# First layer of experts 1 to 7 over two token units at once: 512-column matmuls in place of pairs of 256-column ones

## The chip, the cores and the metric

The kernel runs on one core of a Trainium2 chip. The metric is the device time of one execution in microseconds (us); lower is better. All profile times are from one execution recorded by the hardware profiler. Engines: PE is the matrix engine, PEld its weight load, DVE the vector engine, ACT the scalar engine, POOL GpSimd, SP the sync engine, which here only issues DMAs.

## The reference

Linear attention over 8 batches and 8 heads, 576 positions of 64 numbers, then a mixture of 8 experts in which every token goes through every expert, weighted by a Sinkhorn-balanced matrix P:

```python
q_p, k_p = phi(q), phi(k)                       # phi(x) = elu(x) + 1
kv  = einsum('bhsd,bhse->bhde', k_p, v);  z = sum(k_p, axis=2)
x   = (q_p @ kv) / (q_p . z + 1e-6)             # reshaped to 4608 x 512
P   = exp(x @ w_gate - max)                     # 4608 x 8
for _ in range(8):                              # Sinkhorn
    P /= P.sum(1, keepdims=True) + 1e-9
    P /= P.sum(0, keepdims=True) + 1e-9
    P *= N / E
out = 0
for e in range(8):
    h = relu(x @ w1[e])                         # 512 -> 1024
    out += P[:, e:e+1] * (h @ w2[e])            # 1024 -> 512
```

## The kernel before, in words

**How the order comes about.** Nothing is issued while the program text is read. Every step is a task given to a list scheduler (`_Plan`, L18 to L119) with an engine, an estimated cost, its dependences, a priority, and the buffers that it takes or uses. `S_.run()` then places the tasks engine by engine. Two things written by hand go before that: a table of ranks (`ranks`, L1026 to L1163), which sets priorities and sometimes the engine of single tasks, and a chain of dependences (`order`, `final`, L1009 ff.) that fixes the sequence of PE's products for experts 1 to 7.

**Front.** 16 attention blocks load k, q and v (mostly on SP's queue), compute phi, kv and the quotient, and leave x transposed as `xT` in SBUF, in f16. Sinkhorn runs on PE, DVE and ACT beside expert 0.

**Tokens and experts.** The 4608 tokens are 9 units of 512. For expert 0 the first five units use plain matmuls (layer 1 at L583, layer 2 at L809); the last four units, and all units of experts 1 to 7, use a seven-product scheme in the manner of Strassen for layer 1 (`block7`, L658). Layer 2 of experts 1 to 7 also has seven products (`unit`, L884), apart from the very last unit, whose layer 2 is plain (`unit_plain`, L809, L793).

**The combinations.** The scheme splits the 512 input features and the 512 tokens of a unit in halves. The products need sums of weight blocks (`W`, made by `combos` on DVE, four per expert), and four combinations of x per unit. `x_blocks` (L598 to L636) makes the latter on DVE and writes raw x and combinations to a DRAM tile `xd[g]` with three DMAs on SP (L606, L607, L636). `x_load` (L648) brings 896 KB per unit back as one tile `xs` with one DMA, in two buffers.

**Layer 1 of a unit.** `pair(gi)` is run for gi = 0 and 1. Each has seven products m1 to m7 of four 256-column matmuls (L703): two blocks p of 128 hidden features times two halves c of the contraction. In the order names they are a1 to a7 and b1 to b7; A is the next unit's a. ACT seeds a bank from another (L715), copies two (`s2` L722, `s5` L729) and writes h11 and h21 with relu (L732, L735); DVE writes h12 and h22, an add with relu (L738). m4 waits for h22, as it adds to the same bank.

**Layer 2 of a unit.** Four sums `S` of h on DVE (L900), four sums `T` of w2 per expert (DVE), seven products y1 to y7 of eight 256-column matmuls (L927), and evacuations `acc += P * y`: ten on DVE (L941), two through ACT (L948) and POOL (L951), and a seed copy (L962). In expert 7 finished rows are written out by `out_dma` on SP (L778).

PE's order for unit u in experts 1 to 7, with y of the unit before:

```python
order = "y1 y5 y2 a7 y6 y3 a4 b1 b5 y7 b6 b3 b2 b7 A1 A5 y4 b4 A6 A3 A2".split()
final = "y1 y5 y2 y6 a7 y3 a4 b1 b5 y7 b6 b3 b2 b7 y4 b4".split()
```

Of the kernel before, what the change touches and what calls it, by code (L numbers as in the profile page):

```python
# [122 lines left out]
def kernel(  # L123
# [32 lines left out]
    hpool = ctx.enter_context(tc.tile_pool(name="hpool", bufs=2))  # L156
# [9 lines left out]
    NXB = 7 * 512  # L166
    NL = 4
    NF = 8
    NX = 5
    MG = 99  # L170
    xd = [dpool.tile([P, NXB], FP16, tag=f"xd{g}", name=f"xd{g}") for g in range(NG)]
# [20 lines left out]
    p_T, p_S, p_W, p_xs, p_xst, p_s2, p_s5 = (S_.pool(2) for _ in range(7))  # L192
# [343 lines left out]
    accp = []  # L536
    Zt = [None, None]

    def f_close(_):
        front.close()  # L540
        accp.append(ctx.enter_context(tc.tile_pool(name="accp", bufs=1)))
        for g in range(NA, NG):
            acc[g] = accp[0].tile([P, 4, 512], FP32, tag=f"acc{g}", name=f"acc{g}")
        accp.append(ctx.enter_context(tc.tile_pool(name="combo", bufs=2)))
        zps = ctx.enter_context(tc.tile_pool(name="zps", bufs=1, space=PSUM))
        for i, n in enumerate(("ye2", "ye3")):
            Zt[i] = zps.tile([P, 2, 256], FP32, tag=n, name=f"Z{n}")
# [12 lines left out]
    def layer1(e, g):  # L560
# [6 lines left out]
        def f_ha(_):  # L567
            gh["tile"] = hpool.tile([P, NFT, 512], FP16, tag="h", name="h")
# [29 lines left out]
    def x_blocks(g):  # L598
# [6 lines left out]
        def f_raw(_):  # L605
            nc.sync.dma_start(out=xd[g][:, 0:512].rearrange("p (c t) -> p c t", c=2), in_=xT[:, 0:2, t0:t0 + 256])  # L606
            nc.sync.dma_start(out=xd[g][:, 512:1536].rearrange("p (c t) -> p c t", c=2), in_=xT[:, 2:4, t0:t0 + 512])  # L607
        last = first = None
        for i in range(3):
            def f_T(_, i=i):  # L610
                if i == 0 and early:
                    h_ = (len(p_xse["order"]) - 1) % 2
                    gt_["tile"] = (acc[NA - 1][:, 2 * h_:2 * h_ + 2, :].bitcast(FP16)
                                   .rearrange("p a (b c t) -> p (a b) c t", b=2, c=2))
                elif i == 0:
                    gt_["tile"] = accp[1].tile([P, 4, 2, 256], FP16, tag="xst", name="xst")
# [18 lines left out]
        def f_st(_):  # L635
            nc.sync.dma_start(out=xd[g][:, 1536:NXB], in_=gt_["tile"].rearrange("p i c t -> p (i c t)"))  # L636
# [4 lines left out]
        x_users.append(out_[1])  # L641
# [4 lines left out]
    xst_of, xse_done = {}, []  # L646

    def x_load(e, g):  # L648
        gr = S_.grp(p_xs)

        def fn(_):
            gr["tile"] = accp[1].tile([P, NXB], FP16, tag="xs", name="xs")
            nc.sync.dma_start(out=gr["tile"], in_=xd[g])
        ti = add(("sp", 0.1), fn, acq=[gr], deps=xd_done[g] + [t_close, xs_prev[0]], prio=e * NG + g)
        xs_prev[0] = ti
        return gr, add(("dma", 3.0), lambda _: None, deps=[ti], use=[gr], prio=e * NG + g, lat=2.6)

    def block7(e, g, gW, tW):  # L658
        gw1, tw1, gw2, tw2 = w_t[e]
        ui = e * NG + g  # L660
        gxs, txs = xst_of[g][:2] if e == 0 else x_load(e, g)
        gh = S_.grp(p_h)
        th = [[], []]
        t0 = 512 * g

        def f_ha(_):
            gh["tile"] = hpool.tile([P, NFT, 512], FP16, tag="h", name="h")
        tha = add(("none", 0.0), f_ha, deps=[prev_hq[0]], acq=[gh], prio=ui - 400.0)

        def A(i, j, gi):  # L670
            return lambda p, c: gw1["tile"][:, 2 * (j - 1) + c, ts(4 * (i - 1) + 2 * gi + p, P)]

        def W(i, gi):
            return lambda p, c: gW["tile"][:, i - 1, c, ts(2 * gi + p, P)]

        def Bx(o, w):
            return lambda c: gxs["tile"][:, o + w * c:o + w * c + 256]

        def T(i):
            return Bx(1536 + 512 * (i - 1), 256)  # L680
        B11, B21, B22 = Bx(0, 256), Bx(512, 512), Bx(768, 512)
        if e == 0:
            def Bt(c0, t):
                return lambda c: xT[:, c0 + c, t:t + 256]

            def T(i):
                return lambda c: gxs["tile"][:, i - 1, c, :]
            B11, B21, B22 = Bt(0, t0), Bt(2, t0), Bt(2, t0 + 256)

        def pair(gi):  # L690
            gX, gR, gZ, gs2, gs5 = (S_.grp(p) for p in (p_hq, p_att, p_ye[3], *((p_e2, p_e5) if e == 0 else (p_s2, p_s5))))
            kx = {id(gX): (hqp, "hq"), id(gR): (aps, "att")}
            f0 = 2 * gi

            def pm(lhs, rhs, g_, first, deps, pr):
                def f_m(_):
# [3 lines left out]
                    dst = Zt[1] if g_ is gZ else g_["tile"]  # L700
                    for p in range(2):
                        for c in range(2):
                            nc.tensor.matmul(dst[:, p, :], lhsT=lhs(p, c), rhs=rhs(c),  # L703
                                             start=(first and p == 0 and c == 0), stop=(c == 1), skip_group_check=True)
                return add(("pe", 0.436), f_m, deps=deps, acq=[g_] if first else [], use=[g_, gw1, gW, gxs],
                           prio=ui + (-2.0 if ui == NG else 0.35) + 0.35 * gi + pr)

            def hd(fh, t):
                return gh["tile"][:, 4 * fh + f0:4 * fh + f0 + 2, 256 * t:256 * t + 256]

            def acts(fn, deps, use, acq=()):
                return add(("act", 0.6), fn, deps=deps, use=use, acq=acq, prio=ui - 400.0 + 0.1 * gi)
# [4 lines left out]
            def f_s2(_):  # L717
                if e == 0:
                    gs2["tile"] = acc[NG - 1][:, (len(p_e2["order"]) - 1) % 2, :].rearrange("p (a b) -> p a b", a=2)
                else:  # L720
                    gs2["tile"] = accp[2].tile([P, 2, 256], FP32, tag="s2", name="s2")
                nc.scalar.copy(out=gs2["tile"], in_=gX["tile"])  # L722

            def f_s5(_):
                if e == 0:
                    gs5["tile"] = acc[NG - 1][:, 2 + (len(p_e5["order"]) - 1) % 2, :].rearrange("p (a b) -> p a b", a=2)
                else:
                    gs5["tile"] = accp[2].tile([P, 2, 256], FP32, tag="s5", name="s5")
# [16 lines left out]
            m1 = pm(A(1, 1, gi), B11, gX, True, tw1 + [txs, prev_hq[0], t_zt], 0.0)  # L745
            prev_hq[0] = m1
            a1 = acts(f_seed, [m1], [gX], [gZ])
            m5 = pm(W(1, gi), T(1), gR, True, [m1, tW], 0.05)
            a5 = acts(f_s5, [m5, x_closed[0] if e > 0 else t_close], [gR], [gs5])
            m2 = pm(A(1, 2, gi), B21, gZ, False, [a1], 0.15)  # L750
            th[0].append(acts(f_h11, [m2, tha], [gZ, gh]))
            m6 = pm(W(2, gi), T(2), gX, False, [a1, tW], 0.08)
            a2 = acts(f_s2, [m6, x_closed[0] if e > 0 else t_close], [gX], [gs2])
            m3 = pm(W(4, gi), B22, gR, False, [a5], 0.12)
            th[1].append(add(("dve", 0.69), f_h12, deps=[m3, a2, tha], use=[gR, gs2, gh], prio=ui - 400.0))
            m7 = pm(W(3, gi), T(3), gX, False, [a2], 0.14)
            d22 = add(("dve", 0.69), f_h22, deps=[m7, a5, tha], use=[gX, gs5, gh], prio=ui - 402)
            th[1].append(d22)
            m4 = pm(A(2, 2, gi), T(4), gX, False, [d22], 0.16)
            for n, t in zip("1234567", (m1, m2, m3, m4, m5, m6, m7)):  # L760
                if e == 0:
                    x_users.append(t)
                else:
                    pe_id[(ui, f"{'ab'[gi]}{n}")] = t
            if e > 0:
                pe_id[(ui, f"{'ab'[gi]}22")] = d22
            th[0].append(acts(f_h21, [m4, tha], [gX, gh]))
        pair(0)
        pair(1)
        return gh, th  # L770
# [10 lines left out]
    def unit_plain(e, g, gW=None, tW=None):  # L781
        gw1, tw1, gw2, tw2 = w_t[e]
        gh, th = layer1(e, g) if gW is None else block7(e, g, gW, tW)
        gy = [S_.grp(p_ye[tt % 2]) for tt in range(4)]
        ty = [None] * 4
        cuts = []
        for c in range(2 if e > 0 else 0):
            gc = S_.grp((p_ye[0], p_hq)[c])

            def f_yc(_, c=c, gc=gc):  # L790
                gc["tile"] = (yps, hqp)[c].tile([P, 256], FP32, tag=("ye0", "hq")[c], name="yc")
                for f in range(NFT):
                    nc.tensor.matmul(gc["tile"], lhsT=gh["tile"][:, f, 0:P], rhs=gw2["tile"][:, f, 256 * c:256 * c + 256],  # L793
# [9 lines left out]
        for tt in range(1 if e > 0 else 0, 4):  # L803
            for half in range(2):
                def f_y(_, half=half, tt=tt):
                    if half == 0:
                        gy[tt]["tile"] = yps.tile([P, 512], FP32, tag=f"ye{tt % 2}", name=f"ye{tt % 2}")
                    for f in range(4 * half, 4 * half + 4):
                        nc.tensor.matmul(gy[tt]["tile"], lhsT=gh["tile"][:, f, ds(P * tt, P)], rhs=gw2["tile"][:, f, :],  # L809
# [4 lines left out]
                if e > 0:  # L814
                    pe_id[f"z{tt}{half}"] = ty[tt]
        for c, t in enumerate(cuts):
# [35 lines left out]
    def combos(e):  # L852
        gw1, tw1, gw2, tw2 = w_t[e]
        gT, gW = S_.grp(p_T), S_.grp(p_W)
        tW = tT = None
        if e == 0:
            gT = None
        for i in range(4):
            def f_W(_, i=i):
                if i == 0:  # L860
                    gW["tile"] = accp[1].tile([P, 4, 2, 512], FP16, tag="W", name="W")
                w, W = gw1["tile"], gW["tile"]
                a0, a1, op = [(w[:, 0:2, 512:1024], w[:, 2:4, 512:1024], ALU.add),
                              (W[:, 0], w[:, 0:2, 0:512], ALU.subtract),
                              (w[:, 0:2, 0:512], w[:, 0:2, 512:1024], ALU.subtract),
                              (w[:, 2:4, 0:512], W[:, 1], ALU.subtract)][i]
                nc.vector.tensor_tensor(out=W[:, i], in0=a0, in1=a1, op=op)
            tW = add(("dve", 0.685), f_W, deps=tw1 + [t_close, tW, pe_id.get((NG * (e - 1) + i + 1, "b22"))], acq=[gW] if i == 0 else [], use=[gw1, gW],
                     prio=-900.0 if e > 1 else 4.5)
        for i in range(4 if e > 0 else 0):  # L870
            def f_T(_, i=i):
                if i == 0:
                    gT["tile"] = accp[2].tile([P, 4, 4, 256], FP16, tag="T", name="T")
                w, T = gw2["tile"], gT["tile"]
                a0, a1, op = [(w[:, 0:4, 256:512], w[:, 0:4, 0:256], ALU.subtract),
                              (w[:, 4:8, 256:512], T[:, 0], ALU.subtract),
                              (w[:, 4:8, 256:512], w[:, 0:4, 256:512], ALU.subtract),
                              (w[:, 4:8, 0:256], T[:, 1], ALU.subtract)][i]
                nc.vector.tensor_tensor(out=T[:, i], in0=a0, in1=a1, op=op)
# [321 lines left out]
```

## Time and profile before

| what | value |
|---|---|
| three runs | 962.19, 963.14, 965.29 us |
| median | 963.14 us |
| profiled execution | span 960.4 us from its first to its last instruction; no other time of it is recorded |
| granted PE clock | 1.000 |
| PE busy | 954.2 us (99%), 8833 instructions |
| weight loads on PE | 803.7 us (84%) |
| DVE, ACT, POOL busy | 773.4 us (81%), 572.4 us (60%), 114.1 us (12%) |
| DMA moved | 121.99 MB in 46420 packets |

The span is 2.7 us below the median of the runs. Busy times of PE overlap, since matmuls are pipelined: the cost of a matmul is the distance between the starts of neighbours, not its duration.

### The profile page before, as it was taken

The numbers are of one execution on the slowest core, as the hardware profiler recorded it, in microseconds if no ns is written. First come the engines' busy times: TensorE is split into PE (matmuls) and PEld (weight loads), VectorE is DVE, ScalarE is ACT, GpSimd is POOL, SyncE is SP. The second block draws the span as 40 slices with busy tenths as digits, with TensorE's granted clock in tenths as the row PEclk, the third lists the DMA queues.
The fourth block names the chain that finished last, engine by engine and source line by source line (L and its number), as shares of the span: only waits on it lengthen the run. The fifth ranks groups of instructions, "written<-read, shape, count | busy, mean of one in ns | idle before, by whom it ended". The sixth has DMA issues, their size and how long they took to land.

```text
span 960.4 us, 21585 instructions
## 1 busy us (share of the span) xinstructions
PE 954.2 (99%) x8833; PEld 803.7 (84%) x8833; DVE 773.4 (81%) x1527; ACT 572.4 (60%) x1034; POOL 114.1 (12%) x163
## 2 busy tenths in 40 slices
PE   9999999999999999999999999999999999999998
PEld 4666676688888888888888888888888888888886
DVE  6998889878887888878887888878887888877775
ACT  6897755855555555555555555555555555555553
POOL 4100000011111111111111100111111111111110
PEclk9999999999999999999999999999999999999999
DMA  9987962252227222452227222272226321235554
GB/s 317 345 315 259 277 195 77 44 122 78 78 77 165 78 77 78 113 130 77 78 78 164 79 78 78 81 162 74 68 71 136 93 78 74 78 100 164 166 162 114
DMA packets 46420, 121.99 MB, mean 127 GB/s; under 512 B 4208, under 2 KB 18288, under 8 KB 46320
## 3 DMA queue, kind: packets, MB, share of 16 engines
q1 hardware_dynamic: 30576, 96.22, 30.1%
q0 software_dynamic: 15344, 23.87, 12.9%
q8 instruction: 69, 1.13, 0.5%
q10 hardware_dynamic: 400, 0.52, 0.2%
q14 instruction: 31, 0.25, 0.1%
HBM read 119.69 MB, written 17.69 MB: 143 GB/s over the span
## 4 chain that ended last, share of the span: by engine, by line
PE 95%; DMA 2%; ACT 2%; DVE 0%; issue 0%; POOL 0%; ACTq 0%; DVEq 0%
PE ye L927 34%; PE hq L703 24%; PE att L703 12%; PE ye L809 7%; PE Zye L703 6%; PE Zye L927 6%; PE hq L583 3%; DMA kqin<-in_k_dram 2%; ACT e L285 1%; PE xt_ps L413 1%; PE kv_ps L330 1%; PE num_ps L397 1%; PE qt_ps L358 1%; ACT h L587 0%; PE lg_ps L432 0%; PE den_ps L373 0%
## 5 line engine op out<-in xcount | busy, mean ns | idle before, releaser
L941 DVE SCALAR_TENSOR_TENSOR acc<-ye,P_sb,acc 128x256 f32<-128x256 f32 x620 | 267.3, 479 | 128.1 <-PE ye L927 127.6
L703 PEld LDWEIGHTS <-W 128*128 128x128 f16 x2144 | 209.8, 98 | 26.8 <-issue 0.2
L927 PEld LDWEIGHTS <-S 128*128 128x128 f16 x1984 | 194.1, 98 | 22.5
L927 PE MATMUL ye<-T,S 128*128 128x256 f16 x1488 | 192.8, 273 | 0.0
L703 PEld LDWEIGHTS <-w 128*128 128x128 f16 x1608 | 157.4, 98 | 20.1 <-issue 0.7
L735 ACT ACTIVATE h<-hq 128x512 f16<-128x512 f32 x134 | 80.1, 597 | 146.2 <-PE hq L703 143.3
L951 POOL TENSOR_TENSOR acc<-acc,st 128x256 f32<-128x256 f32 x124 | 87.3, 724 | 619.9 <-ACT st L948 609.2
L927 PEld LDWEIGHTS <-h 128*128 128x128 f16 x1488 | 145.6, 98 | 16.8
L703 PE MATMUL att<-xs,W 128*128 128x256 f16 x1008 | 151.2, 273 | 0.0
L703 PE MATMUL hq<-xs,W 128*128 128x256 f16 x1008 | 151.2, 273 | 0.0
L703 PE MATMUL hq<-xs,w 128*128 128x256 f16 x1008 | 140.9, 273 | 0.3 <-DVE h L738 0.3
L732 ACT ACTIVATE h<-Zye 128x512 f16<-128x512 f32 x134 | 80.1, 598 | 42.6 <-PE Zye L703 42.6
L948 ACT ACTIVATE st<-Zye,P_sb 128x256 f32<-128x256 f32 x124 | 51.9, 470 | 78.0 <-PE Zye L927 78.0
L900 DVE TENSOR_TENSOR S<-h 128x1024 f16<-128x1024 f16 x124 | 85.4, 689 | 13.7 <-ACT h L735 13.7
L738 DVE CUSTOM_DVE_ANT_0 h<-att,s 128x512 f16<-128x512 f32 x126 | 86.7, 688 | 11.7 <-ACT s L722 11.1
L722 ACT COPY s<-hq 128x512 f32<-128x512 f32 x126 | 73.6, 584 | 36.3 <-PE hq L703 36.3
L715 ACT COPY Zye<-hq 128x512 f32<-128x512 f32 x134 | 78.0, 582 | 17.8 <-PE hq L703 17.7
L738 DVE CUSTOM_DVE_ANT_0 h<-hq,s 128x512 f16<-128x512 f32 x126 | 86.7, 688 | 0.6 <-PE hq L703 0.6
L809 PE MATMUL ye<-w,h 128*128 128x512 f16 x312 | 76.6, 379 | 0.0
L703 PE MATMUL Zye<-xs,w 128*128 128x256 f16 x504 | 75.6, 273 | 0.0
L729 ACT COPY s<-att 128x512 f32<-128x512 f32 x126 | 74.6, 592 | 0.0
L927 PE MATMUL ye<-w,h 128*128 128x256 f16 x496 | 64.3, 273 | 0.0
(109 smaller groups left out, 949.7 us busy)
## 6 DMA issues: line engine op xcount, KB each, us to landing
xs<-xd SPq DMA_DIRECT2D x63, 896.0 KB, 4.6
w<-in_moe_w_dram POOLq DMA_DIRECT2D x14, 1024.0 KB, 11.5
out_dram<-acc SPq DMA_DIRECT2D x67, 128.0 KB, 2.4
kqin<-in_k_dram SPq DMA_DIRECT2D x12, 576.0 KB, 5.2
kqin<-in_q_dram SPq DMA_DIRECT2D x12, 576.0 KB, 6.6
vin<-in_v_dram SPq DMA_DIRECT2D x12, 576.0 KB, 7.3
xd<-acc SPq DMA_DIRECT2D x5, 512.0 KB, 4.9
kqin<-in_k_dram POOLq DMA_DIRECT2D x4, 576.0 KB, 10.5
```

The lines of the kernel that those rows point to most:

```text
L703: nc.tensor.matmul(dst[:, p, :], lhsT=lhs(p, c), rhs=rhs(c), start=(first and p == 0 and c == 0), stop=(c == 1), skip_group_check=True)
L715: nc.scalar.copy(out=Zt[1], in_=gX["tile"])
L722: nc.scalar.copy(out=gs2["tile"], in_=gX["tile"])
L729: nc.scalar.copy(out=gs5["tile"], in_=gR["tile"])
L732: nc.scalar.activation(out=hd(0, 0), in_=Zt[1], func=AF.Relu)
L735: nc.scalar.activation(out=hd(1, 0), in_=gX["tile"], func=AF.Relu)
L738: nc.vector._custom_dve(TENSOR_ADD_SAT, out=dst, in0=ps, in1=sb, s0=3.0e38, s1=0.0)
L809: nc.tensor.matmul(gy[tt]["tile"], lhsT=gh["tile"][:, f, ds(P * tt, P)], rhs=gw2["tile"][:, f, :], start=(f == 0), stop=(f == NFT - 1))
L900: nc.vector.tensor_tensor(out=Sx[:, i], in0=a0, in1=a1, op=op)
L927: nc.tensor.matmul(bank(g_)[:, s, :], lhsT=lhs(s, kk), rhs=rhs(kk), start=(new and s == 0 and kk == 0), stop=(kk == 3), skip_group_check=True)
L941: nc.vector.scalar_tensor_tensor(out=dst(), in0=bank(g_)[:, s, :], scalar=P_sb[:, gg, e:e + 1], in1=dst(), op0=ALU.mult, op1=ALU.add)
L951: nc.gpsimd.tensor_tensor(out=dst(), in0=dst(), in1=gst["tile"], op=ALU.add)
```

## The change

- In experts 1 to 7, units 0 to 7 of layer 1 are computed two at a time. A double unit has four pairs instead of two times two. One product of a pair is one block of 128 hidden features (no p loop) times two contraction halves, with 512 columns: 256 tokens of each of the two units. Unit 8 of each expert remains single.
- h of four units is kept in one tile `h4` with four places. Layer 2 stays per unit, but lags two units behind layer 1 instead of one.
- `xd` now holds a pair of units with the seven pieces contiguous. `x_blocks` writes it with seven DMAs per unit (1 + 2 raw, 4 combinations), and `x_load` fetches seven pieces per double unit (256 KB each; 128 KB for unit 8) into a ring of nine tiles.
- `W` and `S` become rings of single tiles (6 and 4), and `T` a ring of 8 in the space that held expert 0's h.
- The last unit's plain layer 2 is interleaved with the seven products of unit 7, and uses other PSUM banks.
- The table of ranks is new, in the front as well.

The core of the diff:

```diff
-    xd = [dpool.tile([P, NXB], FP16, tag=f"xd{g}", name=f"xd{g}") for g in range(NG)]
+    ND = NG // 2
+    xd = [dpool.tile([P, 7, 2, 2 if d < ND else 1, 256], FP16, tag=f"xd{d}", name=f"xd{d}") for d in range(ND + 1)]
...
-    p_T, p_S, p_W, p_xs, p_xst, p_s2, p_s5 = (S_.pool(2) for _ in range(7))
+    p_xst, p_s2, p_s5 = (S_.pool(2) for _ in range(3))
+    p_T, p_W, p_S, p_xs = S_.pool(8), S_.pool(6), S_.pool(4), S_.pool(NXR)
+    p_h4 = [S_.pool(1) for _ in range(4)]
...
         def f_raw(_):
-            nc.sync.dma_start(out=xd[g][:, 0:512].rearrange("p (c t) -> p c t", c=2), in_=xT[:, 0:2, t0:t0 + 256])
-            nc.sync.dma_start(out=xd[g][:, 512:1536].rearrange("p (c t) -> p c t", c=2), in_=xT[:, 2:4, t0:t0 + 512])
+            nc.sync.dma_start(out=xd[g // 2][:, 0, :, g % 2, :], in_=xT[:, 0:2, t0:t0 + 256])
+            for b in range(2):
+                nc.sync.dma_start(out=xd[g // 2][:, 1 + b, :, g % 2, :], in_=xT[:, 2:4, t0 + 256 * b:t0 + 256 * b + 256])
...
         def f_st(_):
-            nc.sync.dma_start(out=xd[g][:, 1536:NXB], in_=gt_["tile"].rearrange("p i c t -> p (i c t)"))
+            for i in range(4):
+                nc.sync.dma_start(out=xd[g // 2][:, 3 + i, :, g % 2, :], in_=gt_["tile"][:, i])
...
     def x_load(e, g):
-        gr = S_.grp(p_xs)
-
-        def fn(_):
-            gr["tile"] = accp[1].tile([P, NXB], FP16, tag="xs", name="xs")
-            nc.sync.dma_start(out=gr["tile"], in_=xd[g])
...
+        d = g // 2
+        out_ = {}
+        for b in (0, 3, 4, 2, 1, 5, 6):
+            gr = S_.grp(p_xs)
+
+            def fn(_, gr=gr, b=b):
+                gr["tile"] = accp[1].tile([P, 2, 2 if d < ND else 1, 256], FP16, tag="xs", name="xs", bufs=NXR)
+                nc.sync.dma_start(out=gr["tile"], in_=xd[d][:, b])
...
                     dst = Zt[1] if g_ is gZ else g_["tile"]
+                    if two:
+                        for c in range(2):
+                            nc.tensor.matmul(dst.rearrange("p a b -> p (a b)"), lhsT=lhs(0, c), rhs=X(b)(c),
+                                             start=(first and c == 0), stop=(c == 1), skip_group_check=True)
+                        return
                     for p in range(2):
                         for c in range(2):
-                            nc.tensor.matmul(dst[:, p, :], lhsT=lhs(p, c), rhs=rhs(c),
+                            nc.tensor.matmul(dst[:, p, :], lhsT=lhs(p, c), rhs=X(b)(c),
                                              start=(first and p == 0 and c == 0), stop=(c == 1), skip_group_check=True)
...
-        pair(0)
-        pair(1)
-        return gh, th
+        for gi in range(4 if two else 2):
+            pair(gi)
+        return ghs, th
...
     def unit(e, g, gW, tW, gT, tT):
...
-        gh, th = block7(e, g, gW, tW)
+        if g % 2 == 0:
+            h_of[0] = block7(e, g, gW, tW)
+        gh, th = h_of[0]
+        gh = gh[g % 2]
...
-    final = "y1 y5 y2 y6 a7 y3 a4 b1 b5 y7 b6 b3 b2 b7 y4 b4".split()
+    final = ("y1 y5 y2 a7 y6 y3 a4 b1 b5 y7 b6 b3 b2 b7 y4 Y1 b4 Y5 Y2 Y6 Y3 "
+             "z30 Y7 z31 z20 Y4 z21 z10 z11 z00 z01").split()
```

(Y is the layer 2 of the unit before the last one, z the plain layer 2 of the last unit.)

## The prediction

> **What bounds the kernel now.** I read the page's first two parts first: does one engine fill the span, and in which slices does it not?
>
> ```profile
> span 960.4 us, 21585 instructions
> PE 954.2 (99%) x8833; PEld 803.7 (84%) x8833; DVE 773.4 (81%) x1527; ACT 572.4 (60%) x1034; POOL 114.1 (12%) x163
> ...
> PE   9999999999999999999999999999999999999998
> ...
> PEclk9999999999999999999999999999999999999999
> DMA  9987962252227222452227222272226321235554
> ```
>
> PE is busy everywhere, at full clock; DVE has a fifth of the span free; the DMA engines are full only in the first five slices (0 to 120 us). A share cannot say whether PE is ever late, so next come the windows (columns: length, then busy time and count of PE, PEld, DVE, ACT, POOL, then clock, DMA share, GB/s):
>
> ```profile
> 0.00:60.00 60.00, 58.31 (x603) 34.11 (x604) 49.26 (x103) 46.39 (x64) 14.23 (x24) 1.00 1.02 332
> 60.00:120.00 60.00, 59.58 (x704) 38.02 (x702) 51.94 (x112) 49.01 (x80) 2.09 (x3) 1.00 0.88 274
> ...
> 450.00:550.00 100.00, 100.00 (x919) 89.63 (x917) 80.94 (x156) 56.67 (x106) 12.98 (x18) 1.00 0.36 103
> ...
> 850.00:960.40 110.40, 106.28 (x948) 92.50 (x946) 79.36 (x153) 56.33 (x106) 11.28 (x16) 1.00 0.54 145
> ```
>
> From 120 us on PE is covered without a hole; the last row's missing 4.1 us is the end (PE stops at 956.6, then the last sum and the write to 960.4). So the chain should be almost all PE, and is:
>
> ```profile
> PE 95%; DMA 2%; ACT 2%; DVE 0%; issue 0%; POOL 0%; ACTq 0%; DVEq 0%
> ...
> L703 PE MATMUL hq<-xs,w 128*128 128x256 f16 x1008 | 140.9, 273 | 0.3 <-DVE h L738 0.3
> ```
>
> The group shows the one wait on another engine behind the front: 0.3 us at the last unit's m4 (a hole of 0.49 us in PE's starts at 943.6), since there nothing stands between m7 and m4 while DVE writes h22. Only fewer or shorter matmuls, or less idle, can move the time. "Mean ns" is no price, as neighbours overlap (273 ns for 256 columns). The price is the pitch, read where matmuls of one width follow each other in the timeline:
>
> ```profile
> 949.08 0.60 PE L703 MATMUL hq<-xs,w 128*128 128x256 f16 x4
> ...
> 949.51 5.34 PE L809 MATMUL ye<-w,h 128*128 128x512 f16 x24
> ...
> 954.69 1.91 PE L793 MATMUL yc<-w,h 128*128 128x256 f16 x16
> ```
>
> 24 matmuls of 512 columns start at 949.51 and the next kind at 954.69: 5.18 / 24 = 215.8 ns. For 256 columns: loads of xs in neighbouring steady units are issued 12.227 us apart, a unit has 112 matmuls: 109.17 ns. Two narrow ones cost 218.34, one wide one 215.85: 2.49 ns less.
>
> **The change, part by part.**
>
> *Matmuls.* The instruction order of the changed kernel has 4104 matmuls of 256 columns and 2089 of 512, against 7240 and 521: 3136 narrow ones become 1568 wide ones (7 experts x 4 double units x 4 pairs x 7 products x 2). 1568 x 2.49 ns = 3.90 us, all of it on the path.
>
> *The end.* In the new `final` the products y4 and Y1 stand between b7 and b4 (0.87 us each; h22 needs 0.69 of DVE), so the 0.49 us hole closes: -0.45. The tail of 3.8 us behind PE is as before. What an undisturbed change gives is therefore 4.35 us and no more: there is no other idle time past 120 us.
>
> *DVE, ACT, POOL.* Same instructions and shapes: S, the adding h, sums and copies. A unit has about 10 us of DVE in 12.2, at the same rate. At an expert's start the W tiles are now made singly, and two (0.69 us each) fall into unit 8, the unit with most DVE work; products m4 wait for h22 with 0.15 to 0.3 us to spare there. Cost: 0 to 0.3 us at 6 boundaries, I take 0.
>
> *xs in pieces.* 63 loads of 896 KB become 245 of 256 KB (128 KB for unit 8), in a ring of 9 tiles. SP's queue holds little else until expert 7. Every issue waits for the product that last read its slot. The tightest is the piece of m2: its slot is free at the end of the last pair's m6, its reader is A2 of the next double unit. Between them stand b3 b2 b7 A1 A5 b4 A6 A3 at 0.432 each and y4 at 0.873: 4.33 us; other pieces have 5.2 and more. The landing is not in the trace for 256 KB read from xd; the nearest rows are the loads it replaces and writes of other sizes:
>
> ```profile
> xs<-xd SPq DMA_DIRECT2D x63, 896.0 KB, 4.6
> ...
> out_dram<-acc SPq DMA_DIRECT2D x67, 128.0 KB, 2.4
> ...
> xd<-xst SPq DMA_DIRECT2D x4, 512.0 KB, 2.8
> ```
>
> Between 128 KB at 2.4 and 896 KB at 4.6, 256 KB comes to 2.4 + 128/768 x 2.2 = 2.8; bounds 2.0 (smallest out landing) and 4.6. With about 0.3 for the semaphore and SP's issue, 2.8 leaves 1.2 us to spare, so I take 0; at 4.6 each of 28 double units would lose 4.6 + 0.3 - 4.33 = 0.6. The Trainium skill, "DMA: Bandwidth & Descriptors", section "Bandwidth", has a rule against this part: batch DMAs to at least 1 MiB. By the fit under "Anatomy of one DMA — SWDGE (gpsimd) path", some 2.0 us fixed plus bytes/436e3, the piece takes 2.6 us, an estimate: splitting is wasteful in bandwidth, but the sum stays at 0.
>
> *Expert 7.* Its out writes share SP's queue, issued 0.5 to 0.7 us apart, up to eight ahead of a run of pieces. Laid out along PE's order, the m2 piece lands about 870.9 and is read at 871.0. Cost 0 to 0.4 at three doubles; I take 0.2 in all.
>
> *The front.* Each x block now issues 7 DMAs on SP, not 3 (its raw halves and four combinations singly, 0.33 to 0.48 us between issues), and they stand ahead of attention inputs on the same queue: v of block 14 behind x block 2, then k, q and v of block 15 behind x block 3. In the trace, v of 14 is issued at 95.95 and lands 6.5 later, and its cast starts at 105.07; k of 15 is issued at 96.70, lands 7.2 later, and the exponential that I match to its last half runs at 107.08. Four more issues put each 1.5 to 1.9 us later, and xd's rows are now 512 bytes throughout: such a packet held a DMA engine 30 ns, a 4096-byte one 167, so a block takes 3.4 us of the 16 engines for 2.6, where they are already full. By that v of 14 lands at 103.0 and k of 15 at 107.5, some 0.8 us after PE's work wants them. The cover is the work of layer 1 that the plan (its ranks are new here too) puts in between; if that is gone the wait grows to 2.5, and a better order may as well gain the front's own idle of about 1. I take +0.8, with -1 and +2.5 as ends.
>
> *From expert 0 to 1.* The Sinkhorn steps end some 11 us later in PE's work, and the first double unit runs among expert 0's second layer. Cost 0 to 1, taken 0.1.
>
> Sum: -3.90 - 0.45 + 0.2 + 0.8 + 0.1 = -3.25. On the profiled span, 960.4 - 3.25 = 957.2; the median 963.14 stands 2.7 above the span, and the same distance gives **959.9 us**. A measurement of this kernel can tell about 0.3%, 2.9 us, from no change: the forecast is just on the far side of that.
>
> **Rivals.**
>
> 1. *The front gives it back.* The two input loads, not layer 1, end last around 100 to 110 us: 2.5 us there and 1 at the start of expert 1, so 4.35 - 3.7 leaves 0.65: 962.5. For: DMA digits of 9 there, and PE's only real holes. Against: 58.31 and 59.58 of 60 show that the plan's spread covers most late landings.
> 2. *The ring of xs decides, and it is slower.* Place: A2 of each double unit. It decides once a piece takes over 4.0 us from issue to landing. At the 4.6 of the big load: 28 x 0.6 - 4.35 + 1.1 = +13.6, 976.7; at 4.2 it would be 28 x 0.2 - 3.25, 965.5. For: a weight load in flight took the 896 KB landing to 6.8 to 7.6. Against: the weight loads of the new order start in unit 8 and beside y4, away from the urgent pieces, and 512 KB landed in 2.8. The skill's rule on batching names such a cost but gives no reason for its size here.
> 3. *The change does not do what it says:* wide matmuls could run slower than 215.8 when reading x over two units and changing weights each time. Pitch equal to two narrow ones leaves -0.45 + 1.1: 963.8. Against: layer 2 of the last unit changes weights each time too (24 PEld to 24 PE).
> 4. *Planned waits turn real on DVE:* h22 late at W boundaries and where two units' h finish together. With 0.15 per double unit (28) and 0.3 at 6 boundaries, +6.0: 965.9. For: spare of only 0.15 to 0.3. Against: DVE is busy 80.94 of 100 and the order of products is unchanged.
>
> **How the numbers follow.** Forecast case (loss 0 to 1.4 us: 958.8 to 960.2): 0.55, with a lucky front down to 958. Rival 1 and rival 3: 0.23 and 0.03, both within 2.9 us. Rival 4: 0.10, split between within and slower. Rival 2: 0.09, slower. Faster 0.55, same 0.30, slower 0.15. The range goes from 958.2 (the undisturbed 958.8 less half of the front's possible gain) to 966.0, which takes in rivals 1, 3 and 4 and the mild end of rival 2.
>
> **What would show it.** Right: spacing of equal products in neighbouring double units down from 24.454 to 24.454 - 56 x 0.00249 = 24.315 us; PE windows of 100.00 from 130 us on; no wait of PE on DVE at the last m4; xs landings near 2.8. Wrong: a releaser "DMA xs" ahead of PE at L703 (rival 2), "DVE h" there (rival 4), PE under 59 of 60 in 60 to 120 us (rival 1), unchanged spacing (rival 3).

## The result, and the profile after

The changed kernel takes 994.9 us (median of 5 runs, 992.38 to 995.89), the kernel before beside it 963.75: ratio 1.0322, interval 1.0307 to 1.0336. It is 3.2% slower where 0.3% faster was forecast, and lies far outside the range of 958.2 to 966.0.

The page of the changed kernel, the same parts as before:

```profile
span 993.0 us, 18857 instructions
...
PE 964.3 (97%) x7265; PEld 654.0 (66%) x7265; DVE 772.7 (78%) x1533; ACT 569.7 (57%) x1027; POOL 126.5 (13%) x163
...
PE   9999999999998999989999999989999899999998
...
PEclk9999999999998999989999899999999999999999
DMA  9997991342155221452245221652215522425545
...
PE 85%; DMA 9%; ACT 4%; DVE 1%; issue 1%; POOL 0%; SPq 0%; DVEq 0%; ACTq 0%
...
L736 PE MATMUL att<-xs,W 128*128 128x512 f16 x448 | 135.0, 383 | 11.9 <-DMA xs<-xd 11.9
...
L736 PE MATMUL Zye<-xs,w 128*128 128x512 f16 x224 | 68.7, 389 | 8.0 <-DMA xs<-xd 8.0
```

Ahead of the end PE's 9s are broken by an 8 in four slices of 24.8 us, and the clock, at 9 everywhere before, in three. Behind these digits lie five holes in PE, at 311, 427, 543, 659 and 774 us, 116 us apart: one in each of experts 2 to 6. 9% of the chain is DMA where it was 2%; the two groups name the transfer. The products are A3 (att, piece 2) and A2 (Zye, piece 1): the place of rival 2. Once per expert, not at every double unit. Around the first (timeline, lines of the queues and of the two products):

```profile
305.27 0.92 POOL L219 DMA_DIRECT2D w<-in_moe_w_dram  x1 [0.40 <-PE ye L996]
...
305.86 5.52 SPq L665 DMA_DIRECT2D xs<-xd  x7
...
310.87 0.59 PE L736 MATMUL hq<-xs,W 128*128 128x512 f16 x2
...
314.23 1.03 PE L736 MATMUL att<-xs,W 128*128 128x512 f16 x2 [2.76 <-DMA xs<-xd]
...
315.70 1.01 PE L736 MATMUL Zye<-xs,w 128*128 128x512 f16 x2 [0.44 <-DMA xs<-xd]
...
316.51 1.91 PE L996 MATMUL ye<-w,h 128*128 128x256 f16 x8
```

At 305.27 POOL issues the 1 MB load of w2 for the next expert, at 305.86 SP begins the seven pieces. The product at 310.87 is A6, the next starts at 314.23. Then eight 256-column matmuls of L996 take 1.91 us where they took 1.04. Windows of PE with the granted clock (length, PE busy and count, clock, DMA share, GB/s) show why:

```profile
308.00:311.30 3.30, 3.30 (x20) 1.00 1.03 162
311.30:314.20 2.90, 0.16 (x1) 0.95 1.16 277
314.20:316.50 2.30, 1.83 (x4) 0.50 1.14 284
316.50:318.00 1.50, 1.50 (x8) 0.50 1.09 339
318.00:319.00 1.00, 1.00 (x6) 0.50 0.45 156
...
321.00:322.00 1.00, 1.00 (x10) 1.00 0.00 0
```

The DMA engines are full, PE stands, and from 313.9 to 320.8 us the clock is 0.50 (of full speed), although PE is busy again from 315.7 on. The load itself takes 13.9 us to land. The landings of the run of seven pieces beside the load, and of the next run without one (summary lines of the tile xs in the two windows):

```profile
DMA to landing us min/median/max: 3.3/9.0/10.1
```

```profile
DMA to landing us min/median/max: 2.7/3.5/4.0
```

In the kernel before, an xs load issued at 302.0, with the w2 load of 296.17 still in flight, also took long, 6.9 us, and PE's windows there were full: the two whole buffers gave it a unit, 12.2 us, of lead. The ring of nine pieces gives 4.33 us.

**The sum.** Below, idle means the start-to-start distance of PE's matmuls beyond the pitch at full clock, added up, so slow matmuls count in it too. From the profile before to the one after it grows by 3.5 us up to 124 us (5.3 to 8.8), by 30.4 from 200 to 860 (1.0 to 31.4), by 2.1 in expert 7 (0.7 to 2.8), and shrinks by 0.4 between 124 and 200; 0.6 more lies behind PE's end; the matmuls save 3.9. That gives 32.3, and the spans differ by 32.6. Of the five holes' 30 us, the waits are 20.2 (2.9 + 0.9, 4.0 + 0.6, 3.1 + 1.0, 2.5 + 0.9, 4.3) and the rest, 10, is work at the lower clock.

### The profile page after: what moved, and what is told of

Same layout as the page of the kernel before. It is cut to its first block, busy times and chain, and to the rows that moved or that the text cites. A ratio compares the mean times of both kernels' runs of the same rounds, so it can differ in the third digit from the quotient of the medians.

```text
span 993.0 us, 18857 instructions
## 1 busy us (share of the span) xinstructions
PE 964.3 (97%) x7265; PEld 654.0 (66%) x7265; DVE 772.7 (78%) x1533; ACT 569.7 (57%) x1027; POOL 126.5 (13%) x163
## 4 chain that ended last, share of the span: by engine, by line
PE 85%; DMA 9%; ACT 4%; DVE 1%; issue 1%; POOL 0%; SPq 0%; DVEq 0%; ACTq 0%
PE ye L996 33%; PE hq L736 18%; PE att L736 9%; PE Zye L996 6%; DMA xs<-xd 5%; PE Zye L736 5%; PE ye L858 5%; PE hq L741 4%; DMA kqin<-in_k_dram 2%; PE att L741 2%; DMA kqin<-in_q_dram 1%; ACT e L290 1%; PE hq L590 1%; PE Zye L741 1%; ACT acc L887 1%; ACT h L594 1%
## 5 line engine op out<-in xcount | busy, mean ns | idle before, releaser
L996 PEld LDWEIGHTS <-S 128*128 128x128 f16 x1984 | 195.5, 99 | 47.5 <-issue 0.2
L996 PE MATMUL ye<-h,S 128*128 128x256 f16 x1488 | 195.8, 275 | 0.0
L1020 POOL TENSOR_TENSOR acc<-acc,st 128x256 f32<-128x256 f32 x124 | 100.3, 829 | 636.8 <-ACT st L1017 636.8
L996 PEld LDWEIGHTS <-h 128*128 128x128 f16 x1488 | 148.0, 99 | 44.2 <-issue 3.2
L736 PEld LDWEIGHTS <-W 128*128 128x128 f16 x896 | 87.4, 98 | 93.8 <-DMA xs<-xd 13.8
L736 PE MATMUL att<-xs,W 128*128 128x512 f16 x448 | 135.0, 383 | 11.9 <-DMA xs<-xd 11.9
L736 PE MATMUL hq<-xs,W 128*128 128x512 f16 x448 | 133.2, 379 | 0.0
L736 PE MATMUL hq<-xs,w 128*128 128x512 f16 x448 | 124.1, 379 | 0.0
L736 PEld LDWEIGHTS <-w 128*128 128x128 f16 x672 | 66.0, 98 | 65.3 <-issue 11.9
L756 ACT COPY Zye<-hq 128x512 f32<-128x512 f32 x134 | 77.9, 581 | 19.9 <-PE hq L736 13.9
L736 PE MATMUL Zye<-xs,w 128*128 128x512 f16 x224 | 68.7, 389 | 8.0 <-DMA xs<-xd 8.0
L996 PE MATMUL ye<-w,h 128*128 128x256 f16 x496 | 68.3, 284 | 0.0
```

What stands on the lines that cost most here:

```text
L736: nc.tensor.matmul(dst.rearrange("p a b -> p (a b)"), lhsT=lhs(0, c), rhs=X(b)(c), start=(first and c == 0), stop=(c == 1), skip_group_che ...
L756: nc.scalar.copy(out=Zt[1], in_=gX["tile"])
L996: nc.tensor.matmul(bank(g_)[:, s, :], lhsT=lhs(s, kk), rhs=rhs(kk), start=(new and s == 0 and kk == 0), stop=(kk == 3), skip_group_check=True)
L1020: nc.gpsimd.tensor_tensor(out=dst(), in0=dst(), in1=gst["tile"], op=ALU.add)
```

## The experiments

**1. The weight load moved.** Only the time at which w2 is loaded changes, about one unit later; PE's order stays the same, and this w2 isn't needed before the next expert. The dependence is added to the one line, here cut:

```diff
-... + load_w2(e, prio=float(e), deps=w_t[e - 1][3][1:])
+... + load_w2(e, prio=float(e), deps=w_t[e - 1][3][1:] + [pe_id[(NG * (e - 1) + 0, "y4")]])
```

> The w2 load of experts 2 to 7 is made to wait for y4 of unit 0 of the expert before, one unit (about 12.2 us) later than now; nothing else is changed. Theory (the weight load slows the pieces): in the changed kernel the 1 MB load is released by y4 of unit 8 at the moment at which the seven pieces of the second double unit are issued; those then take 7.5 to 10 us to land, not 3 to 4, and PE stands in front of A3 and A2 and then runs at a clock of 0.5. Moved away, the five holes at 311, 427, 543, 659 and 774 us (30.2 us of idle between 300 and 800 us) go: 994.9 - 30.2 = 964.7 us. Rival (the ring of single pieces is late by itself at the first turn after the single unit): the holes stay, 990 us or more. In between, some 975, if the moved load now meets the pieces of the third double unit.

Measured: 963.16 us, ratio to the kernel before 0.9994 (0.9985 to 1.0004): 31.7 us below the changed kernel. Its page, and the landings of the run of pieces at the place of the first hole:

```profile
span 961.3 us, 18857 instructions
...
PE   9999999999999999999999999999999999999998
...
PEclk9999999999999999999999999999999999999999
```

```profile
DMA to landing us min/median/max: 2.8/3.8/4.5
```

The holes between 200 and 860 us are gone (idle there 1.2 us for 31.4), and the clock stays at 9. One dependence on one load takes away 30.2 of the 31.7 us by which the two spans differ; the rest is in the front and in expert 7. That the kernel is still no faster than the one before is the front (7.9 us of idle for 5.3 in the first profile), expert 7 (2.2 for 0.7) and the end (0.5 more): together they use up the 3.9 us of the matmuls.

**2. The load moved to the next run of pieces.** The same edit with `NG * (e - 1) + 1`.

> As the run with the late w2 load, but the load waits for y4 of unit 1 in place of unit 0: two units later than in the changed kernel, and so again at the moment at which a run of seven pieces is issued, now those of the third double unit. Theory (weight load and pieces at one time): the holes are back, one turn later (some 336, 452, 568, 684 and 800 us), 963.2 + 30 = 993 us. Rival (only the first turn after the single unit is short of time, and any later load is harmless): 963 to 967 us.

Measured: 998.12 us, ratio 1.0364 (1.0348 to 1.038). Six holes, one turn later: expert 1 has one too. Timeline at the second:

```profile
340.60 0.59 PE L736 MATMUL hq<-xs,w 128*128 128x512 f16 x2
342.90 0.61 PE L736 MATMUL hq<-xs,W 128*128 128x512 f16 x2 [1.70 <-DMA xs<-xd]
344.28 1.03 PE L736 MATMUL att<-xs,W 128*128 128x512 f16 x2 [0.78 <-DMA xs<-xd]
345.79 1.01 PE L736 MATMUL Zye<-xs,w 128*128 128x512 f16 x2 [0.47 <-DMA xs<-xd]
```

So it is not the first turn after the single unit that matters: in both places in which load and pieces met, the pieces were late. Expected were five holes and 993 us; the sixth, some 5 us, makes up the rest.

**3. The wait filled with useless work.** The product A5 ahead of the hole is computed eleven times. Below, `rpt` is set for that one product in experts 2 to 6 (second double unit, first pair).

```diff
-                        for c in range(2):
+                        for c in (0, 1) * (11 if rpt else 1):
```

> In experts 2 to 6 the product A5 of the second double unit is computed eleven times over (each time from the start of the bank, so the value is the same): 20 more matmuls of 512 columns, 4.3 us of useless work per expert, right ahead of the place where PE now stands and waits. Theory (half of the loss is the clock): a hole is some 3.8 us of waiting and some 2.3 us of slow matmuls behind it, because the granted clock falls to 0.5 after the wait. With the wait filled the clock stays at 1.0; each hole costs 4.3 us in place of about 6.0: 994.9 - 5 x 1.8 = 986 us, faster by doing more work. Rival (the clock costs nothing, the whole loss is waiting for transfers): 4.3 us of work replaces 4.3 us of waiting, 995 us. Rival (the transfer is released by PE's progress and moves along with it): 994.9 + 5 x 4.3 = 1016 us.

Measured: 985.24 us, ratio 1.0219 (1.0201 to 1.0237). 100 more wide matmuls (21.6 us of PE) make the kernel 9.7 us faster than the changed one. In the windows of the first hole PE has work, and the clock never drops:

```profile
311.30:314.20 2.90, 2.90 (x17) 1.00 1.15 272
314.20:316.50 2.30, 2.08 (x13) 1.00 1.13 277
316.50:318.00 1.50, 1.26 (x10) 1.00 1.07 328
```

This shows that the lower clock is a cost of its own, about 2 us per hole on top of the wait, and that the late pieces do not move along with PE.

**4. Expert 7's output writes on POOL.** All but the last unit's go from SP's queue to POOL's.

> The writes of finished rows of units 0 to 7 in expert 7 are issued by POOL and not by SP. Theory (SP's queue): the two holes in expert 7 (1.34 and 1.17 us ahead of A2 at 913.4 and 939.1) come from two output writes that SP issues between two pieces (1.1 us); they go, 992.4 us. Rival (the writes share the DMA engines, and that alone makes pieces late): both holes stay, 994.9 us.

Measured: 989.97 us, ratio 1.0271 (1.0254 to 1.0288), 4.9 us below the changed kernel. SP's queue ahead of the first of the two holes in the changed kernel, and in this run:

```profile
908.67 1.02 SPq L665 DMA_DIRECT2D xs<-xd  x2
909.80 1.11 SPq L819 DMA_DIRECT2D out_dram<-acc  x2
911.00 2.53 SPq L665 DMA_DIRECT2D xs<-xd  x5
```

```profile
902.91 5.52 SPq L665 DMA_DIRECT2D xs<-xd  x7
```

Idle behind 860 us falls from 2.79 to 0.62: the two holes of expert 7 are gone, so they came from SP's queue. The rest of the 4.9 us is another matter. PE's end to the span's end is 2.0 us longer (6.4 for 4.4) and the front idles 0.9 more, but idle from 200 to 860 us is 25.6 us in place of 31.4. PE's order is the same there, and the waits in the holes are hardly shorter (18.5 us for 20.2); the clock was at 0.50 for 13.7 us in place of 27.3. The last section says on what that hangs.

**5. The front with the ranks of before.** Tasks up to expert 0's end are the same in both kernels, so the old table can be used for them.

> The ranks of all tasks up to expert 0's end are those of the kernel before (these tasks are the same in both); the rest is the changed kernel. Theory A (the new order costs the front 3.4 us): PE's idle beyond the pitch up to 120 us falls from 8.7 back to 5.3 us, 991.5 us. Theory B (the seven DMAs per x block delay the attention inputs on SP's queue): the order changes nothing, 994 to 996 us, and the waits stay at DMA landings.

Measured: 996.93 us, ratio 1.0328 (1.0298 to 1.0358): no gain. Idle up to 124 us is 6.9, but between 124 and 200 us it grows from 0.8 to 4.4, perhaps because the old order fits the old start of expert 1. Neither theory is shown.

**6. The kernel before, a second time.**

> The kernel before, unchanged, for a second profile: how much PE's idle up to 124 us moves between executions. If the 5.3 us of the first profile is typical: 4.8 to 5.8 us, and the 7.9 to 10.0 us of the new order is its own. If the front moves by chance: up to 8 us.

Measured: span 963.3 us, device time 965.07. Windows:

```profile
0.00:60.00 60.00, 58.14 (x600) 34.05 (x601) 48.58 (x101) 45.83 (x63) 14.33 (x24) 1.00 1.02 331
60.00:120.00 60.00, 57.68 (x662) 36.13 (x660) 51.05 (x110) 47.70 (x77) 2.19 (x3) 1.00 0.83 260
```

PE has 57.68 of 60 where the first profile had 59.58; idle up to 124 us is 8.2, not 5.3. So the front of the very same program moves by 3 us, and the 8.8 of the changed kernel (7.9 to 10.0 in five more profiles with the same front) is too little to show a loss. Measured against this profile the front costs 0.6 us. This execution also has both times, 1.8 us apart.

**7. Both repairs together:** the late w2 load and the writes on POOL.

> The late w2 load (y4 of unit 0) and the output writes of units 0 to 7 on POOL, together. Theory (SP's queue makes the last two holes): the 0.76 and 1.24 us in expert 7 go, 963.2 - 2.0 = 961.2 us, just below the kernel before. Rival (the tail or POOL takes it back, as POOL's sums wait behind its DMA issues): 963 us.

Measured: 966.02 us, ratio 1.0011 (1.0000 to 1.0022). Neither expectation was met. Expert 7's holes are gone (idle 0.65), yet no gain: this profile's front has 10.0 us of idle (the clock was at 0.50 there too, for 3.4 us from 60.0 us on), and the last writes on POOL make the stretch from PE's end to the span's end 6.4 us (957.6 to 964.0), where the run with the late load has 4.4.

**8. One DMA for four combinations** in each x block.

```diff
-            for i in range(4):
-                nc.sync.dma_start(out=xd[g // 2][:, 3 + i, :, g % 2, :], in_=gt_["tile"][:, i])
+            nc.sync.dma_start(out=xd[g // 2][:, 3:7, :, g % 2, :].rearrange("p i c t -> p (i c) t"),
+                              in_=gt_["tile"].rearrange("p i c t -> p (i c) t"))
```

> The run before with the four combinations of each x block written by one DMA and not by four (same 512-byte rows): four DMAs per block in place of seven. Theory (SP's issues delay the attention inputs): PE's idle up to 124 us falls from about 8.5 to some 6 us, 959 us. Rival (the front is lost to the new order or to the small rows): unchanged, 961.2 us.

Measured: 964.09 us, ratio 1.0002 (0.9993 to 1.0011), 1.9 below the run before, the intervals overlapping. Idle up to 124 us was 7.1. By the second profile of before, this size is within chance: inconclusive.

**9. The DRAM tile unit by unit**, written in long rows and read as two rows of 1024 bytes.

> The run before with the DRAM tile laid out unit by unit: the four combinations are written in rows of 4096 bytes, the raw halves in dense rows of 1024; the pieces are then read as two rows of 1024 bytes and the moving operand of the wide matmul has two segments. Theory (small rows load the full DMA engines in the front): a further 1 us less idle up to 124 us, 958 us. Rival (issue count or order alone): as the run with one DMA for four. Rival (1024-byte rows or the segmented operand slow the steady part): holes ahead of A2, or a pitch over 215.9 ns; above 961 us.

Measured: 968.72 us, ratio 1.0046 (1.0033 to 1.0059), slower. The front is no better (8.7). But an issue on SP now takes a median of 524 ns, not 362, and the pieces land later (xs between 250 and 860 us, here and in experiment 7):

```profile
L665 SPq DMA_DIRECT2D xs<-xd x196: 319/524/1339, 250.4 to 859.9; - x196
...
DMA to landing us min/median/max: 2.0/3.7/7.1
```

```profile
L665 SPq DMA_DIRECT2D xs<-xd x197: 319/362/1354, 251.4 to 859.8; - x197
...
DMA to landing us min/median/max: 2.0/3.2/6.1
```

Some 0.16 us more for each issue and half a microsecond more for the landing are enough: PE waits for piece 1 at four A2 (4.4 us in all), 1.1 us of it ahead of 422.5 us, where its run of pieces landed in 5.3 (median) with no weight load in flight. The operand in two segments is not to blame: wide matmuls still start 215.8 ns apart. The ring has no more to spare than the prediction reckoned.

**10. The best of these:** late w2 load, one DMA for four combinations, writes of units 0 to 5 on POOL and of 6 and 7 on SP.

> The late w2 load, one DMA for the four combinations of an x block, and the output writes of units 0 to 5 on POOL, those of 6 and 7 back on SP. Theory (POOL's writes at the end made the tail 6.2 us in place of 4.4, while those between the pieces belong to units 1 to 5): 964.1 - 1.8 = 962.3 us, 0.2% below the kernel before. Rival (the front decides and moves by 1 to 2 us between runs): 963 to 965 us.

Measured: 962.45 us, ratio 0.9977 (0.9968 to 0.9987): 0.2% faster than the kernel before, and 32 us faster than the change as it was made.

## Why the prediction was wrong, point by point

*Matmuls, right.* In the run with the late load, the product A2 or its like recurs every 24.313 us in neighbouring steady double units; 24.315 was forecast. The 3.90 us are there.

*The end, right in its main term.* The wait of the last m4 is gone. But the tail behind PE is 4.4 us, not 3.8, perhaps as the writes of unit 7 queue up with those of unit 8; no run shows it.

*xs in pieces: the step that failed.* The sum took 0, and rival 2 was put at 0.09 with "the weight loads of the new order start in unit 8 and beside y4, away from the urgent pieces". The order line itself has y4 between A5 and b4, with A6, A3 and A2 right behind: y4 is not away from the urgent pieces but at their issue (load at 305.27, first piece at 305.86). The slack (4.33 us) and the point of decision (a landing over 4.0) were right: without the load the runs of pieces shown landed in 3.5 and 3.8 us (medians) and, in the run with the late load, no product of experts 2 to 6 waited; beside it they landed in 8.6 to 9.7, and A3 and A2 together waited 3.4 to 4.7 us. The landing price of 2.8 was low for a run of seven (3.5), but did no harm. What was mis-sized in rival 2 is the count and the size of the stall: 5 x 6.0 us, not 28 x 0.6. The 6.8 to 7.6 us of the old load beside a weight load was quoted as "for" the rival, and its price never put into the sum. A landing of 7.6 would have given 7.6 + 0.3 - 4.33 = 3.6 us per expert.

*The clock: missing from the sum.* Each hole cost 2 us more than its wait, on average. The Trainium skill, "TensorE: Matmul & The Clock Gate", section "HAM oscillation — how this bites in real kernels", says that idle gaps of PE beyond some 3.4 us bring the clock down to half. The trace agrees with the half (0.50), and experiment 3 with the remedy of keeping PE at work. It does not agree on the length: at 311 us the clock fell 2.6 us after PE stood.

*Expert 7: right mechanism, size off.* 0.2 us was taken with 0.4 each as bound; two output writes between pieces made 1.3 and 1.2 us.

*The front: not decidable at its size.* +0.8 was taken; the same program's front varies by 3 us. The reasons given with it were partly false. The ranks of the first 501 tasks are unchanged. And the two input loads were to be issued 1.5 to 1.9 us later; in the profile after they are issued 5.5 and 9.2 us later (v of block 14 at 101.45, k of block 15 at 105.85), and still PE's idle grew by only 3.5 us against one profile of the kernel before and 0.6 against the other.

*The distance of the times.* 2.7 us was taken between span and device time; executions that have both show 1.8 to 2.1. The profile before thus belongs to an execution of some 962.2 to 962.5 us, the low end of its runs.

*Rivals.* Rival 2 named the engine, the transfer, one of the two products (A2) and the sign, and gave 976.7 us, 18 us short. The sign set for rival 1, PE under 59 of 60 us from 60 to 120 us, came (58.13), but the kernel before shows it as well in its second profile (57.68), so it decides nothing. Rivals 3 and 4 fell: the pitch is reached, and no wait of PE on h shows.

## What to carry to other kernels

When a prefetch of a whole buffer becomes a ring of small pieces, the lead falls from one buffer time to the gap between the freeing read and the next use; put every other large transfer on that time line, by the order of the instructions that release it. A transfer that isn't urgent should be released by something that lies right behind the urgent ones. A stall of PE is worth its length and the slower work behind it: waits of 4 us cost 6 here.

## What was not expected of the hardware

The clock does not need one long wait. In experiment 2 the waits at 341, 343 and 345 us are 1.86, 0.94 and 0.89 us with matmuls between them, and still (windows of PE, clock in the third column from the end):

```profile
342.00:343.00 1.00, 0.10 (x1) 1.00 1.16 285
343.00:344.00 1.00, 0.51 (x2) 0.92 1.14 286
344.00:345.00 1.00, 0.72 (x2) 0.50 1.13 278
...
349.00:350.00 1.00, 1.00 (x6) 0.50 0.02 6
350.00:351.00 1.00, 1.00 (x8) 0.67 0.00 0
```

It falls some 2.8 us after PE first stood and returns 6.8 us later; in the hole at 311 us it fell after 2.6 us and also returned after 6.8. Waits of 1.0 to 1.6 us standing alone (experiment 9, expert 7) left it at 1.00.

The traces' own records of the clock show on what this hangs. In every profile here its changes lie whole multiples of 3.413 us apart, so 0.50 lasts 3.4 or 6.8 us. Lay that grid over the profiles of the changed kernel and its variants, from 200 us on, and take for each step the share of time in which no matmul's pitch runs. At full clock, all 19 steps idle for 68% or more before PE's end were followed by 0.50, and none idle for 63% or less was; at 0.50 the clock came back behind every step idle for up to a quarter and behind none idle for more than 26%. So the phase of a wait against the grid counts beside its length: the last hole of experiment 2 (803 to 807 us) has 3.9 us of waits, more than the 3.7 at 341 us, but they fall on two steps, idle for 63% and 51%, and the clock stayed at 1.00. That the chip decides by such steps is an inference from these records.
